# An attention and soft-MoE kernel on one core: norm steps, small operations, turned loads and the order of the last stage rearranged

## The chip, the core and the metric

The kernel runs on one core of a Trainium2 chip. The metric is the device time of one execution in microseconds (us). The kernel before was run three times beside the profile: 319.63, 318.76 and 318.81 us, a median of 318.81 us. Engines go by the names of the profile: PE (TensorE matmuls), PEld (its weight loads), DVE (VectorE), ACT (ScalarE), POOL (GpSimd) and SP (SyncE, which here only issues DMAs).

## What is computed

The inputs are q, k and v of 4 batches, 5056 rows, 256 columns, all fp32, and the weights of a soft mixture of 8 experts with 4 slots each. The attention is over columns: q and k are divided by the norm of each column, and the scores are a 256 x 256 matrix per batch.

```python
qn = q / (np.linalg.norm(q, axis=1, keepdims=True) + 1e-06)
kn = k / (np.linalg.norm(k, axis=1, keepdims=True) + 1e-06)
s = kn.transpose(0, 2, 1) @ qn / tau
a = np.exp(s - s.max(-1, keepdims=True)); a /= a.sum(-1, keepdims=True) + 1e-09
x = (v @ a).reshape(20224, 256)
logits = x @ phi                      # 32 slots
d = softmax(logits, axis=0)           # over all 20224 rows
slot_in = d.T @ x                     # 32 x 256
slot_out[e] = np.maximum(slot_in[e] @ w1[e], 0) @ w2[e]
out = softmax(logits, axis=1) @ slot_out
```

## The kernel before

**Chunks and half chunks.** Each batch's rows are cut into 5 chunks of 1024 rows (the last has 960), and q and k are handled in half chunks of 512 rows: u counts them, 10 per batch, 40 in all. v is handled in whole chunks: y counts those, 5 per batch, 20 in all; y = 12 to 14 are the last three of batch 2 and 15 to 19 are batch 3. In the names of the traces v2_3 is chunk 3 of batch 2.

**Scores (`score`, L194).** For each half chunk, PE adds k'q into a PSUM tile S of the batch. A half chunk has 4 row blocks. In `n_split(u)` of them (L117) q and k are split into a high and a low fp32r part: ACT casts the high part (`cast`, L171), DVE subtracts to get the low part (`split`, L176), and PE runs three fp32r matmuls. The other blocks go to PE as plain fp32 (the profile counts two passes for each of those matmuls). ACT squares the half chunk (`square`, L182) and DVE sums the squares into `all` (`add`, L184 to L192).

**Norms and attention (`attention`, L222).** At a batch's end DVE folds `all` to `sum` (L229, L230), PE sums it over partitions (`nn`, L234), ACT copies the result, POOL takes the root and adds 1e-6 (L244, L245), DVE inverts (L247), POOL multiplies in 1/tau (L250), ACT makes a diagonal matrix `dg`, PE spreads it over partitions (`rq`, L258), and DVE scales a copy of the scores, `ssb` (L264). Then come the row maximum (L267), exp (`a`, L270), a transpose (`aTp`, `aT`) and the product with phi: `Mp`, scaled to `M` (L288, L298). M turns rows of v straight into logits, so no logit of a batch exists before its M.

**Chunks of v (`slots`, L518).** M needs v with its columns on partitions. For that PE transposes half chunks of v (128 columns each; two per chunk, m = 0 and 1): 8 transposes into two PSUM tiles `vTp` (L311), evicted to `vT` by ACT (L322) and in the last stage also by DVE (L320). For 12 of the 40 half chunks (m = 1 of y = 0 to 11) the kernel instead loads a copy of v that the host has laid out with columns first (`load_turned`, L155, tiles vD). PE then makes the logits L (L335), and ACT copies them to `lt` (L346). In the last chunk of a batch DVE first sets rows that don't exist to -1e30 in L itself (L331).

**The running softmax over rows (`chain`, L359).** Per group of 3 or 2 chunks: DVE takes the maximum (L372, or L350 per chunk in batch 3), POOL (DVE in batch 3) folds it over partitions and with the earlier maximum to `negm` (L380 to L401), ACT takes exp (L413), DVE transposes to `dn` (L429), and PE multiplies with v into G (L458). At a batch's end G goes through `a` to `acc` (L478 to L516).

**What sets the order.** The instructions of PE, DVE, ACT and SP stand in the order in which the Python code issues them. A loop over u issues cast, add, score, square and split, and lets generators (`attention`, `slots`, `chain`) take one step at each `advance`; a generator yields the letter of the engine of its next step (E: a big DVE step, one per advance). Chunk y starts at u = LAG + 2y = 16 + 2y. After u = 39 the remaining chunks, y = 12 to 19, are worked off in the same manner, two at a time.

**Loads.** All DMAs are issued by SP in order, so an issue that waits for its buffer holds up all that stand behind it. q and k have 5 raw buffers; v has 6; turned half chunks have 3. From u = 16 on, each chunk of v is issued right behind the half chunks of q and k of the same step. The chunks y = 14 to 18 go into buffers that q and k leave (tag r), then come the weights w1 and w2 of the experts, into buffers that squares, splits and v leave.

**The end.** When batch 3's G is complete, the slots go through the experts (`up` H L691, `flip_h`, `down` O L717), and the output stage (L763 on) multiplies the row softmax with the result, evicts it and stores 20.71 MB.

## Time and profile before

| | us |
|---|---|
| median of three runs | 318.81 |
| the profiled execution's own time | 321.6 |
| its span, first to last instruction | 318.6 |
| PE busy | 291.1 |
| DVE busy | 234.6 |
| ACT busy | 208.2 |
| POOL busy | 49.0 |
| DMA queue, share of 16 engines' span | 85.3% |

The page of a profile sums up one execution. Its windows give, for each stretch, each engine's busy time with the count of instructions, then the granted PE clock (1.00 is full), the mean busy share of the 16 DMA engines, and GB/s. A timeline row gives start, duration, engine, line and names, count, and in brackets the idle time ahead of it and whose result ended it. PE's matmuls are pipelined and their ends are modelled, so the time that a run of matmuls takes is read from the start of one row to the start of the next. Busy time is no proof of a bound: the stage and what is waited for in it decide.

### The profile page before, as it was taken

Reading aid. Unit: us, or ns where it says so; the run is one execution under the profiler, and the core shown is the slowest. Engines: PE = TensorE matmul, PEld = TensorE weight load, DVE = VectorE, ACT = ScalarE, POOL = GpSimd, SP = SyncE. Lnnn points to the kernel's source line nnn. Section 1 sums busy time; section 2 is a strip of 40 time slices with the busy share of each in tenths; the row PEclk is TensorE's granted clock in tenths of the full one; section 3 lists DMA queues with packets and bytes.
Section 4 is the critical chain, followed back from the end, with each engine's and each line's share of the span. In section 5 each row is a group of like instructions: output and inputs, shape, how many; then the busy total and the mean of one; then the engine's idle time right before and its main releaser. Section 6 shows DMA issues by size and latency. Waiting matters only on the chain.

```text
span 318.6 us, 5880 instructions
## 1 busy us (share of the span) xinstructions
PE 291.1 (91%) x2224; PEld 227.2 (71%) x2224; DVE 234.6 (74%) x342; ACT 208.2 (65%) x313; POOL 49.0 (15%) x94
## 2 busy tenths in 40 slices
...
GB/s 294 418 334 348 338 338 255 408 366 413 411 413 384 376 212 419 412 413 388 414 223 236 391 419 400 382 74 338 255 196 422 46 2 263 397 426 399 421 406 292
DMA packets 23468, 106.25 MB, mean 334 GB/s; under 512 B 3216, under 2 KB 4240, under 8 KB 17424
## 3 DMA queue, kind: packets, MB, share of 16 engines
q1 hardware_dynamic: 23440, 105.89, 85.3%
...
q14 instruction: 11, 0.09, 0.1%
HBM read 85.17 MB, written 20.71 MB: 332 GB/s over the span
## 4 chain that ended last, share of the span: by engine, by line
PE 69%; DVE 10%; ACT 7%; issue 5%; DMA 2%; POOL 1%; SPq 1%; ACTq 0%; DVEq 0%; POOLq 0%
PE S L213 33%; PE vTp L311 6%; PE L L335 6%; PE G L458 6%; PE op L786 4%; PE op L787 4%; ACT sq L182 3%; DMA raw<-in_k_dram 2%; PE O L717 2%; PE cTp L775 2%; PE Mp L288 1%; PE nn L234 1%; DVE all L192 1%; DVE nat L650 1%; DVE cm L653 1%
## 5 line engine op out<-in xcount | busy, mean ns | idle before, releaser
L213 PE MATMUL S<-raw 128*128 128x256 f32 x368 | 87.2, 390 | 0.0
L213 PEld LDWEIGHTS S<-raw 128*128 128x128 f32 x368 | 69.4, 194 | 16.1 <-issue 6.1
L182 ACT ACTIVATE sq<-raw 128x2048 f32<-128x2048 f32 x40 | 76.4, 1911 | 4.7 <-DVE all L190 4.7
L192 DVE TENSOR_TENSOR all<-all,sq 128x2048 f32<-128x2048 f32 x32 | 73.1, 2284 | 8.4 <-ACT sq L182 8.2
L176 DVE TENSOR_TENSOR hl<-raw,hl 128x1024 fp32r<-128x1024 f32 (+1 forms) x39 | 42.3, 1085 | 22.0 <-ACT hl L171 22.0
L213 PE MATMUL S<-hl 128*128 128x256 f32 x408 | 56.2, 290 | 1.0 <-DVE hl L176 0.9
L213 PEld LDWEIGHTS S<-hl 128*128 128x128 f32 x408 | 51.1, 191 | 2.6 <-DVE hl L176 1.4
L171 ACT CAST hl<-raw 128x1024 fp32r<-128x1024 f32 (+1 forms) x39 | 36.5, 936 | 17.2 <-PE S L213 9.3
L311 PE MATMUL vTp<-ident,v 128*128 128x128 f32 x224 | 31.0, 285 | 3.9 <-ACT vT L322 3.0
L786 PE MATMUL op<-soh,cT 128*128 128x512 f32 x80 | 32.8, 410 | 0.7 <-ACT cT L780 0.7
L311 PEld LDWEIGHTS vTp<-ident,v 128*128 128x128 f32 x224 | 25.8, 145 | 10.6 <-issue 3.7
L790 ACT COPY o<-op 128x512 f32<-128x512 f32 x53 | 29.0, 606 | 5.4 <-PE op L787 5.4
L787 PE MATMUL op<-sol,cT 128*128 128x512 f32 x80 | 31.6, 395 | 0.0
L322 ACT COPY vT<-vTp 128x512 f32<-128x512 f32 x40 | 21.8, 584 | 14.5 <-PE vTp L311 14.5
L335 PE MATMUL L<-vT,M 128*32 128x256 f32 (+1 forms) x224 | 18.7, 426 | 6.0 <-DVE L L331 4.5
L458 PE MATMUL G<-v,dn 128*32 128x256 f32 x320 | 21.8, 396 | 1.5 <-DVE dn L429 1.5
L792 DVE COPY o<-op 128x512 f32<-128x512 f32 x27 | 18.4, 687 | 4.9 <-PE op L787 4.7
L244 POOL TENSOR_TENSOR rn<-rn,half 128x4 f32<-128x4 f32 x4 | 10.3, 2565 | 60.8 <-ACT rn L243 60.8
L320 DVE COPY vT<-vTp 128x512 f32<-128x512 f32 x16 | 11.0, 689 | 10.1 <-PE vTp L311 9.9
L786 PEld LDWEIGHTS op<-soh,cT 128*128 128x128 f32 x80 | 15.0, 188 | 4.4 <-ACT cT L780 1.4
L787 PEld LDWEIGHTS op<-sol,cT 128*128 128x128 f32 x80 | 15.1, 188 | 3.0
L458 PEld LDWEIGHTS G<-v,dn 128*32 128x32 f32 x320 | 9.5, 112 | 9.9 <-issue 3.1
...
## 6 DMA issues: line engine op xcount, KB each, us to landing
...
v<-in_v_dram SPq DMA_DIRECT2D x16, 1024.0 KB, 10.4
...
```

Of the source, the lines that this page charges most:

```text
L171: nc.scalar.copy(hl[u][:, 0, :, :ns], raw_of(u)[:, :, :ns])
L176: nc.vector.tensor_tensor(hl[u][:, 1, :, :ns], raw_of(u)[:, :, :ns], hl[u][:, 0, :, :ns].bitcast(F32), op=ALU.subtract)
L182: nc.scalar.activation(sq[u], raw_of(u), AF.Square)
L192: nc.vector.tensor_tensor(st[b]["all"], st[b]["all"], sq.pop(u), op=ALU.add)
L213: nc.tensor.matmul(sps[:, m, :], lhs, rhs, start=r == 0 and part == 0 and x == 0 and y == 0 and m == 0, stop=r == H - 1 and part == 1 and ...
L311: nc.tensor.transpose(tp[:, jj, :], vt[:, 4 * hh + jj, P * m : P * m + P], ident)
L322: nc.scalar.copy(dst, st[b]["tp", ch, m, hh])
L335: nc.tensor.matmul(L[S * g : S * g + S, :je, :], M[:, m, :], st[b]["vT", ch, m][:, :je, S * g : S * g + S], start=m == 0, stop=m == 1,)
L458: nc.tensor.matmul(gp[S * g : S * g + S, :], tiles[c][:, j, :], vt[:, j, :], start=c == 0 and j < G, stop=c == n - 1 and j >= G,)
L786: nc.tensor.matmul(op, cT[:, jj, :], soh, start=True, stop=False)
L787: nc.tensor.matmul(op, cT[:, jj, :], sol, start=False, stop=True)
L790: nc.scalar.copy(od, op)
```

## The change

In the order of the program:

- **Splits.** u = 0 and 1 have no split block; from u = 20 on, half chunks with even u have 3 split blocks and odd ones 2 (before: 2 in all of them). Over all u that is 76 instead of 68.
- **Turned loads.** 23 half chunks instead of 12 come turned from memory: both halves of y = 0 to 2, and m = 1 of all others, so also in the last stage. The tiles vD have 4 buffers, and m = 0 of y = 0 to 2 goes into the buffers of vT.
- **Issue order on SP.** Every load has a key in units of u and the list is sorted by it. The first six chunks of v are issued at u = 4, 7, 10, 13, 16 and 19, the later ones at LAG + 2y - 4. Chunks start two half chunks earlier (LAG is 14), so 13 of them start before the scores end.
- **Norms.** DVE's folding of the squares is issued behind the last `add` of its own batch, and `add(u)` follows in the same step u. S is no longer copied: DVE reads it in PSUM, with `rq` as a copy in SBUF. 1/tau sits in the matrix `tones` by which PE spreads `rq`. Of POOL's small steps only the root is left; adding 1e-6 and 1e-9 goes to DVE.
- **Running softmax.** POOL's folding of the maximum goes to DVE, the spreading of `negm` over partitions to ACT, and the two subtractions go into ACT's exp.
- **Rows that don't exist.** POOL writes -1e30 into `lt`, and ACT copies only real rows there. DVE no longer writes to L.
- **The last stage.** `settle` picks the next step by a little model of three engine clocks and of when each generator is ready; PSUM banks for logits and transposes are counted in `busy`, and batch 3 uses a second bank for logits of odd chunks. The five chunks of batch 3 all go into the r buffers, with its turned half chunks and w1_1 to w1_4 between them.

In the diff, TURN gives the halves of chunk y that come turned, LAG the u at which chunk 0 starts, RB the raw buffers, V0 and VS the first key and the spacing of the early loads of v, and LW the w1 loads behind each late chunk.

```diff
+    TURN = lambda y: (0, 1) if y < 3 else (1,)
     VB = 6
     HP = 150
     CUT = [(0, 2), (2, 4), (4, 8)]
     LATE = {2: 1, 3: 6}
-    AHEAD = 0
+    LAG = 14
+    WIDE = 2
+    BIAS = (0, 0, 0, 0)
+    LW = (0, 0, 1, 1, 2)
+    RB = 5
+    LEAD = 4
+    LEADV = 4
+    V0 = 4
+    VS = 3
...
-    NS = 2
+    NS = 3
     H = 2 * NCH
 
     def n_split(u):
-        return 0 if u == 0 else (1 if u < 2 * H and u % 2 else NS)
+        return {0: 0, 1: 0, 2: 1}[u] if u < 3 else (1 if u < 2 * H and u % 2 else 2 if u < 2*H or u%2 else 3)
...
-    def load_qk(b, ch):
-        r = []
...
+    def load_qk(u):
+        b, r = divmod(u, H)
+        ch, h = divmod(r, 2)
+        raw = apool.tile([P, 2, HJ, C], F32, tag="raw", name=f"raw{b}_{ch}_{h}", bufs=RB)
...
-        x = bpool.tile([P, J, P], F32, tag="vD", name=f"vD{b}_{ch}_{m}", bufs=3)
+        x = bpool.tile([P, J, P], F32, tag="vD" if m else "vT", name=f"vD{b}_{ch}_{m}", bufs=4 if m else 3)
...
-        ssb = bpool.tile([P, 2, C], F32, tag="ssb", name=f"ssb{b}")
-        nc.scalar.copy(ssb, st[b]["S"])
-        yield "E"
...
-        nc.gpsimd.tensor_scalar_add(rn, rn, 1e-6)
         yield "D"
+        nc.vector.tensor_scalar_add(rn, rn, 1e-6)
         nc.vector.reciprocal(rn, rn)
-        rk = bpool.tile([P, 2], F32, tag="rk", name=f"rk{b}")
-        for i in range(2):
-            nc.gpsimd.tensor_scalar_mul(rk[:, i : i + 1], rn[:, 2 + i : 3 + i], rtau)
...
-        nc.tensor.matmul(rq[:, :C], ones, dg, start=True, stop=True)
+        nc.tensor.matmul(rq[:, :C], tones, dg, start=True, stop=True)
+        yield "A"
+        rqs = bpool.tile([P, C], F32, tag="dg", name=f"rqs{b}")
+        nc.scalar.copy(rqs, rq[:, :C])
         yield "D" if last else "E"
+        while not st[b].get("scored"):
+            yield "~E"
...
-                ssb[:, m, :], ssb[:, m, :], rk[:, m : m + 1], rq[:, :C], op0=ALU.mult, op1=ALU.mult
+                ssb[:, m, :], st[b]["S"][:, m, :], rn[:, 2 + m : 3 + m], rqs, op0=ALU.mult, op1=ALU.mult
...
-        L = pb.tile([P, 2, J, S], F32, tag="L", name=f"L{b}_{ch}")[:, 0]
+            st[b]["mxs", lo] = bpool.tile([P, 3], F32, tag="mxs", name=f"mxs{b}_{ch}", bufs=2)
+        tag = "amisc" if b == B - 1 and ch % 2 else "L"
+        L = pb.tile([P, 2, J, S], F32, tag=tag, name=f"L{b}_{ch}")[:, 0]
         if ch == NCH - 1:
-            nc.vector.memset(L[TL:, JL, :], -1e30)
+            nc.gpsimd.memset(st[b]["lt", lo][TL:, ch - lo, JL, :], -1e30)
...
-        nc.scalar.copy(st[b]["lt", lo][:, ch - lo], st[b]["L", ch])
+        to, L = st[b]["lt", lo][:, ch - lo], st[b]["L", ch]
+        if ch == NCH - 1:
+            nc.scalar.copy(to[:, :JL], L[:, :JL])
+            nc.scalar.copy(to[:TL, JL], L[:TL, JL])
+        else:
+            nc.scalar.copy(to, L)
...
+    def turn_logits(b, lo, hi):
+        nc.vector.transpose(
+            nat[b][:, lo * J : hi * J, :].rearrange("p j s -> p (j s)"),
+            st[b]["lt", lo][:, : hi - lo].rearrange("p c j s -> p (c j s)"),
+        )
+        run["lt"] -= 1
+        yield from ()
...
-                nc.gpsimd.tensor_scalar_mul(mx[:, g : g + 1], mxs[S * g : S * g + S, 0:1], -1.0)
-        if not final:
-            yield "D"
-        nc.vector.tensor_reduce(mx[:, G:], mx[:, :G], axis=AX.X, op=ALU.min)
+                nc.vector.tensor_scalar_mul(mx[:, g : g + 1], top, -1.0)
...
-            if start:
-                tiny.tensor_copy(to, mx[:, G:])
-            else:
-                tiny.tensor_scalar_min(to, mx[:, G:], before[:S])
+        before, ended = run.get("negm"), run.get("ended")
+        if start:
+            nc.vector.tensor_reduce(negm[:S], mx[:, :G], axis=AX.X, op=ALU.min)
+        else:
+            nc.vector.tensor_reduce(mx[:, G:], mx[:, :G], axis=AX.X, op=ALU.min)
+            nc.vector.tensor_scalar_min(negm[:S], mx[:, G:], before[:S])
         run["negm"] = negm
+        if end:
+            run["ended"] = negm
+        yield "A"
+        for g in range(1, G):
+            nc.scalar.copy(negm[S * g : S * g + S], negm[:S])
...
+            while run["vT"] > 2 or ("T", second_bank(ch)) in busy:
+                yield "~P"
+            bank = "T", second_bank(ch)
+            run["vT"] += 1
+            busy.add(bank)
...
+        if b == B - 1:
+            lo = groups[b][gi][0]
+            scan(b, ch, st[b]["mxs", lo][:, ch - lo : ch - lo + 1])
+            if ch < NCH - 2:
+                to_nat(b, ch)
...
+    def settle(todo, wide):
+        cost = {"P": 0.9, "A": 0.65, "D": 0.6, "E": 1.0}
+        clock = dict.fromkeys("PAD", 0.0)
+        ready = {}
+        spins = 0
+        while todo or active:
+            while todo and sum(x[0] == 2 for x in active) < wide:
+                start_after(slots(*todo.pop(0)), 2, "P")
+            now = min(clock.values())
+            spins = spins + 1
+            assert spins < 3000, [(x[0], x[2].__name__, x[3], x[2].gi_frame.f_lineno, {k: v for k, v in x[2].gi_frame.f_locals.items() if k in ("b", "ch", "gi")}) for x in active]
+
+            def when(x):
+                return max(ready.setdefault(x[1], now), clock["D" if x[3][0] == "E" else x[3][0]])
+
+            x = min(active, key=lambda x: (when(x) + BIAS[x[0]], x[0], x[1]))
+            t, tag, n = when(x), x[3], x[1]
+            if hop(x):
+                ready[n] = t + 0.3
+            else:
+                end = t + (float(tag[1:]) if tag[1:] else cost[tag[0]])
+                clock["D" if tag[0] == "E" else tag[0]] = end
+                ready[n] = end + 0.25
...
+    loads = [(u - RB, 0, load_qk, (u,)) for u in range(B * H)]
+    loads += [(0.5, 1, load_small, ()), (2 * WI, 1, nc.sync.dma_start, (w1t[0], w1[0].rearrange("(p d) f -> p d f", d=2)))]
+    for y in range(NCH * (B - 1)):
+        b, ch = divmod(y, NCH)
+        for m in TURN(y):
+            loads.append((LAG + 2 * y - LEAD + m, 2, load_turned, (b, ch, m)))
+        loads.append((V0 + VS * y if y < VB else LAG + 2 * y - LEADV, 3, load_v, (b, ch)))
+    for key, _, f, args in sorted(loads, key=lambda x: x[:2]):
+        f(*args)
...
+        add(u)
+        if r == H - 1:
+            start_after(attention(b), 0, "E")
         score(u, 0)
         advance("PAD")
-        square(u)
+        if u == 0:
+            square(u)
         if u + 1 < U:
+            square(u + 1)
             split(u + 1)
         score(u, 1)
+        if r == H - 1:
+            st[b]["scored"] = True
...
+    late_w1 = iter(range(1, E))
+    for ch in range(NCH):
+        load_v(b, ch, big("r", f"v{b}_{ch}"))
+        for t in ["w"] * LW[ch]:
+            load_w1(next(late_w1), t)
+        for m in TURN(NCH * b + ch):
+            load_turned(b, ch, m)
+    for e in late_w1:
+        load_w1(e, "v")
...
-        w2t[e] = big(f"w2_{e}")
+        w2t[e] = big("v" if e < E - 5 else "r", f"w2_{e}")
...
-    todo = list(rest)
-    while todo or active:
-        if todo and sum(x[0] == 2 for x in active) < 2:
-            start_after(slots(*todo.pop(0)), 2, "P")
-        advance()
+    settle(list(rest), WIDE)
```

Three places show the move. The first is DVE in batch 2, around u = 22 to 26 (all2 sums squares, hl25 is the split of u = 25, dn0_0 and nat0 are the transposes of batch 0's first group). Before:

```order
L176 TENSOR_TENSOR hl25_981<-raw2_2_1_219,hl25_981 128x1024
L429 STREAM_TRANSPOSE dn0_0_1021<-et0_0_978 128x768
L433 COPY zacc_111<-z0_0_977 128x1
L192 TENSOR_TENSOR all2_883<-all2_883,sq24_1000 128x2048
L283 RECIPROCAL sm1_973<-sm1_973 128x2
L331 MEMSET L0_4_1045 64x32
L176 TENSOR_TENSOR hl26_1027<-raw2_3_0_228,hl26_1027 128x1024
L440 STREAM_TRANSPOSE nat0_106<-lt0_0_717 128x768
```

Now the same stretch reads:

```order
L200 TENSOR_TENSOR all2_855<-all2_855,sq22_889 128x2048
L184 TENSOR_TENSOR hl23_904<-raw2_1_1_224,hl23_904 128x2x512
L272 SCALAR_TENSOR_TENSOR ssb1_949<-S1_519,rn1_837,rqs1_902 128x256 x2
L275 TENSOR_REDUCE nm1_951<-ssb1_949 128x2
L200 TENSOR_TENSOR all2_855<-all2_855,sq23_928 128x2048
L184 TENSOR_TENSOR hl24_969<-raw2_2_0_227,hl24_969 128x1536
L291 TENSOR_SCALAR sm1_952<-sm1_952 128x2
L292 RECIPROCAL sm1_952<-sm1_952 128x2
L379 STREAM_TRANSPOSE nat0_107<-lt0_0_663 128x768
```

The MEMSET of L0_4, which stood behind an addition of squares, is gone from DVE, and the splits of even u have 1536 elements a row instead of 1024.

The second is PE from the norm sums of batch 3 (nn3) on. Before:

```order
L234 MATMUL nn3_1824<-ones_84,sum3_1759 128x1 x4
L311 MATMUL vTp2_2_0_0_1830<-ident_79,v2_2_307 128x128 x4
L311 MATMUL vTp2_2_0_1_1835<-ident_79,v2_2_307 128x128 x4
L487 MATMUL gtp1_1844<-fold_96,gs1_1671 128x32 x2
L311 MATMUL vTp2_2_1_0_1850<-ident_79,v2_2_307 128x128 x4
L311 MATMUL vTp2_2_1_1_1855<-ident_79,v2_2_307 128x128 x4
L311 MATMUL vTp2_3_0_0_1860<-ident_79,v2_3_309 128x128 x4
L311 MATMUL vTp2_3_0_1_1865<-ident_79,v2_3_309 128x128 x4
L311 MATMUL vTp2_3_1_0_1886<-ident_79,v2_3_309 128x128 x4
L311 MATMUL vTp2_3_1_1_1891<-ident_79,v2_3_309 128x128 x4
L258 MATMUL rq3_1896<-dg3_1874,ones_84 128x256
L511 MATMUL sp1_1898<-a1_971,gts1_1877 32x256 x2
```

Now:

```order
L239 MATMUL nn3_1800<-ones_84,sum3_1796 128x1 x4
L324 MATMUL vTp2_3_0_0_1877<-ident_79,v2_3_318 128x128 x4
L324 MATMUL vTp2_3_0_1_1882<-ident_79,v2_3_318 128x128 x4
L324 MATMUL vTp2_4_0_0_1903<-ident_79,v2_4_322 128x128 x4
L324 MATMUL vTp2_4_0_1_1908<-ident_79,v2_4_322 128x128 x4
L260 MATMUL rq3_1916<-dg3_1897,tones_105 128x256
L471 MATMUL G2_0_1922<-v2_0_291,dn2_0_1913 32x256 x8
L349 MATMUL L2_3_1935<-vT2_3_0_1900,M2_1569 32x256 x4
L349 MATMUL L2_3_1935<-vD2_3_1_320,M2_1569 32x256 x4
L471 MATMUL G2_0_1922<-v2_1_301,dn2_0_1913 32x256 x8
L349 MATMUL L2_4_1962<-vT2_4_0_1919,M2_1569 32x256 x2
```

Between nn3 and the first products G2_0 stood sixteen tiles of transposes, and M of batch 3 (Mp3); now four tiles stand there, and Mp3 comes behind G2_0. nn3 still stands behind the last score matmul of its batch.

The third is SP, the last loads of batch 1. Before:

```order
L141 DMA raw1_3_1_176<-in_q_dram 128x1024
L141 DMA raw1_3_1_176<-in_k_dram 128x1024
L159 DMA vD0_0_1_179<-in_v_rows_dram 128x1024
L152 DMA v0_0_181<-in_v_dram 128x2048
L141 DMA raw1_4_0_183<-in_q_dram 128x1024
L141 DMA raw1_4_0_183<-in_k_dram 128x1024
L141 DMA raw1_4_1_186<-in_q_dram 128x768
L141 DMA raw1_4_1_186<-in_q_dram 64x256
L141 DMA raw1_4_1_186<-in_k_dram 128x768
L141 DMA raw1_4_1_186<-in_k_dram 64x256
L159 DMA vD0_1_1_192<-in_v_rows_dram 128x1024
L152 DMA v0_1_194<-in_v_dram 128x2048
```

Now:

```order
L150 DMA raw1_2_1_175<-in_k_dram 128x1024
L167 DMA vD0_0_0_178<-in_v_rows_dram 128x1024
L160 DMA v0_2_180<-in_v_dram 128x2048
L150 DMA raw1_3_0_182<-in_q_dram 128x1024
L150 DMA raw1_3_0_182<-in_k_dram 128x1024
L167 DMA vD0_0_1_185<-in_v_rows_dram 128x1024
L150 DMA raw1_3_1_187<-in_q_dram 128x1024
L150 DMA raw1_3_1_187<-in_k_dram 128x1024
L167 DMA vD0_1_0_190<-in_v_rows_dram 128x1024
L150 DMA raw1_4_0_192<-in_q_dram 128x1024
L150 DMA raw1_4_0_192<-in_k_dram 128x1024
L167 DMA vD0_1_1_195<-in_v_rows_dram 128x1024
```

These rows held two turned half chunks and two chunks of v; now they hold four and one, and v0_0 and v0_1 stand further up, between loads of batches 0 and 1. A raw load is still issued when the raw buffer of five half chunks earlier comes free, and everything that stands ahead of it is moved first.

166 lines of the change are left out of this document (66 added, 100 removed).

## The prediction

> **What bounds the kernel now.** I read the windows first, cut at the stage ends that PE's timeline shows: scores of batches 0 to 3, the last chunks, the experts, the output. A row gives the stretch and its length, busy time (and instructions) of PE, PEld, DVE, ACT and POOL, the granted clock, the DMA share and GB/s.
>
> ```profile
> 0.00:41.00 41.00, 38.39 (x191) 32.23 (x192) 28.64 (x28) 27.50 (x23) 1.22 (x7) 1.00 0.92 347
> 41.00:81.00 40.00, 39.45 (x262) 35.07 (x261) 34.01 (x27) 31.94 (x38) 9.22 (x7) 1.00 0.94 358
> 81.00:132.10 51.10, 49.23 (x391) 40.35 (x390) 40.26 (x38) 39.80 (x52) 13.93 (x24) 0.97 0.96 372
> 132.10:187.30 55.20, 53.60 (x464) 42.28 (x463) 43.44 (x43) 39.94 (x54) 17.01 (x29) 1.00 0.92 354
> 187.30:241.90 54.60, 46.03 (x480) 31.26 (x478) 31.47 (x92) 20.45 (x57) 7.65 (x27) 0.91 0.74 292
> 241.90:259.00 17.10, 16.71 (x210) 7.81 (x211) 12.32 (x25) 6.67 (x11) 0.00 (x0) 1.00 0.35 146
> 259.00:318.60 59.60, 47.74 (x242) 38.15 (x241) 44.42 (x94) 41.86 (x80) 0.00 (x0) 0.94 0.86 348
> ```
>
> Up to 187.3 PE is busy 96 to 99% of four stages and the DMA engines 92 to 96%: PE bounds, with the loads close behind. From 187.3 to 241.9 nothing is full: this stage waits. From 241.9 on the change touches nothing of weight, so I carry 318.6 - 241.9 = 76.7 us over.
>
> Next, what a step costs PE. These rows of PE's timeline are one half chunk and its neighbours in batch 2.
>
> ```profile
> 88.08 3.72 PE L213 MATMUL S<-raw 128*128 128x256 f32 x16
> 91.64 1.04 PE L311 MATMUL vTp<-ident,v 128*128 128x128 f32 x8
> 92.43 3.12 PE L213 MATMUL S<-hl 128*128 128x256 f32 x24
> 95.39 0.59 PE L258 MATMUL rq<-dg,ones 128*128 128x256 f32 x2
> 95.91 0.64 PE L335 MATMUL L<-vT,M 128*32 128x256 f32 x8
> 96.36 0.61 PE L335 MATMUL L<-vD,M 128*32 128x256 f32 x8
> 96.91 3.72 PE L213 MATMUL S<-raw 128*128 128x256 f32 x16
> ```
>
> From start to start, 16 plain passes take 3.56 us (0.2225 each), 24 split matmuls 2.96 (0.123), the transposes of a half chunk 0.79, the logits of a chunk 1.00.
>
> Then the waits in that stage: first two rows of DVE, then five of PE.
>
> ```profile
> 104.06 2.29 DVE L192 TENSOR_TENSOR all<-all,sq 128x2048 f32<-128x2048 f32 x1
> 106.44 0.09 DVE L331 MEMSET L<- 64x32 f32 x1
> ...
> 106.67 1.05 PE L335 MATMUL L<-vT,M 128*32 128x256 f32 x8 [1.87 <-DVE L L331]
> 107.42 1.16 PE L335 MATMUL L<-vD,M 128*32 128x224 f32 x8
> 108.50 2.78 PE L213 MATMUL S<-raw 128*128 128x256 f32 x8
> 111.12 0.97 PE L288 MATMUL Mp<-phi_sb,aT 128*128 128x32 f32 x8
> 161.61 0.62 PE L335 MATMUL L<-vT,M 128*32 128x256 f32 x8 [1.60 <-DVE L L331]
> ```
>
> A memset of 0.09 us stood behind an addition of 2.29 us, and PE waited 1.87 us for it, 1.60 us again in the next batch. After the first wait 108.50 - 106.67 = 1.83 us went on logits that cost 1.00 elsewhere, and 2.62 on 8 plain passes that cost 1.78: 1.7 us of slow clock.
>
> **Stage one, to the norm sums of batch 3 (187.3 before).**
> - Splits: 76 blocks instead of 68. That is 32 plain passes less (7.1 us) and 48 split matmuls more (5.9): -1.2 on PE.
> - Chunks: 13 instead of 12 fall into the stage, so +1.0 of logits; transposed half chunks fall from 12 to 10 (y = 0 to 2 need none): -1.6.
> - The memset goes to POOL and into lt, and PE no longer waits for DVE there: -(1.87 + 1.60 + 1.7) = -5.1. What is late next there is the eviction of lt by ACT, which PE's following logits need a whole half chunk later.
> - More on DVE and ACT. From u = 20 on, the split of even u grows from 1024 to 1536 elements:
>
> ```profile
> L176 DVE TENSOR_TENSOR hl<-raw,hl 128x1024 fp32r<-128x1024 f32 x29 | 35.5, 1223 | 15.1 <-ACT hl L171 15.1
> L176 DVE TENSOR_TENSOR hl<-raw,hl 128x512 fp32r<-128x512 f32 x10 | 6.9, 686 | 6.9 <-ACT hl L171 6.9
> L391 DVE TENSOR_SCALAR negm<-mx,negm 32x1 f32<-32x1 f32 x8 | 1.6, 204 | 0.2
> ```
>
> 512 elements more cost 1.223 - 0.686 = 0.54 us. Per batch the small steps taken over from POOL are some twelve at 0.204: 2.4 us. A pair of half chunks in batch 3 has 43.44/5 = 8.7 us of DVE; now 8.7 + 0.54 + 0.5 = 9.7. PE's pair is 3.56 + 2.96 + 0.79 + 1.00, 1.00 for G, and some 0.8 for attention (estimated from matmuls like the seven rows above), 10.1, now 9.95 by 12 plain passes and 30 split matmuls. DVE still fits, with 3% left, so some of its waits will reach PE: bounds 0 (it fits) and +5 (0.5 us on each of the ten pairs). I take +1, near the lower end, because squares now stand a half chunk ahead of their additions. ACT, at 39.94/5 = 8.0, has room for what it gets.
> - Loads that are late. Of the share-weighted rates, 358/0.94 = 381, 372/0.96 = 388 and 354/0.92 = 385: 385 GB/s is what the engines moved when full. Up to the half chunk u = 24 SP now issues 25 x 1.05 MB of q and k, 5 chunks of v and 7 turned halves of 0.52, 35.1 MB: 91 us at that rate, and 3 for the idle 8% of the first 41 us, so 94. Its cast stands at the start of half chunk 23, the second half of the split matmuls from 92.43: 93.9, less 3 x 0.79 is 91.5. Late by 2.5. Bounds: 0 at 400 GB/s, +7.7 at 365. Later in the stage a pair asks 3.67 MB per 10 us, 367 GB/s, and the lead grows again.
>
> Sum: -1.2 + 1.0 - 1.6 - 5.1 + 1 + 2.5 = -3.4, so 183.9.
>
> **The last chunks (54.6 us before).** This view is PE, ACT and DVE on the way to M, then to the experts.
>
> ```profile
> 190.06 0.18 DVE L247 RECIPROCAL rn<-rn 128x4 f32<-128x4 f32 x1
> 193.72 0.86 DVE L264 SCALAR_TENSOR_TENSOR ssb<-ssb,rk,rq 128x256 f32<-128x256 f32 x2
> ...
> 201.96 2.55 PE L311 MATMUL vTp<-ident,v 128*128 128x128 f32 x12 [1.77 <-ACT vT L322]
> 204.30 1.75 PE L288 MATMUL Mp<-phi_sb,aT 128*128 128x32 f32 x8
> 230.75 1.06 PE L335 MATMUL L<-vT,M 128*32 128x256 f32 x16 [1.00 <-DVE L L331]
> 241.86 5.36 PE L691 MATMUL H<-w,slT 128*32 128x512 f32 x48 [0.30 <-DVE slT L669]
> 253.51 5.39 PE L717 MATMUL O<-w,hT 128*32 128x256 f32 x96
> ...
> 206.09 0.47 ACT L298 ACTIVATE M<-Mp,sm 128x32 f32<-128x32 f32 x2 [1.81 <-PE Mp L288]
> ```
>
> The clock in it, in two windows, and the length of three steps:
>
> ```profile
> 204.00:208.00 4.00, 3.91 (x27) 2.62 (x25) 2.12 (x5) 0.76 (x4) 0.53 (x1) 0.50 0.61 252
> 208.00:212.00 4.00, 3.59 (x33) 1.40 (x33) 1.16 (x3) 0.73 (x2) 1.29 (x6) 0.50 0.01 4
> ```
>
> ```profile
> L429 DVE STREAM_TRANSPOSE dn<-et 128x768 f32<-128x768 f32 x3 | 2.9, 971 | 0.0
> L270 ACT ACTIVATE a<-ssb,nm 128x256 f32<-128x256 f32 x8 | 4.0, 503 | 0.6 <-DVE nm L267 0.6
> L413 ACT ACTIVATE et<-lt,negm 128x768 f32<-128x768 f32 x3 | 2.8, 935 | 4.8 <-POOL negm L391 2.9 <-POOL negm L389 1.9
> ```
>
> - To M: 206.5 - 187.3 = 19.2 us. nn still stands behind the last score and the root is still on POOL: rn inverted at 190.06 - 187.3 + 0.18 = 2.9, now 2.6 with one hop less. dg ends at 3.5, rq at 4.0. DVE has dn (0.97), nat (0.97) and two evictions of vT (0.69) ahead of ssb, so it starts at 6; ssb 0.9, nm 0.7 and a 1.1 end at 8.7. On ACT the eviction of L2_3, that of L2_4, and behind a new maximum the exp of batch 2's second group stand ahead of aT: 14.2. aT 0.6, Mp 0.8, M 0.5: 16.2 instead of 19.2, so -3. Less PE work is in the way, but ACT's queue takes its place.
> - M to the last logits: 231.8 - 206.5 = 25.3. Of 16 transposed half chunks in the whole stage 7 are left. Behind M now stand two products G (1.00 each, like logits), five logits, three transposed half chunks (2.4) and 1 of small matmuls: 10.4, plus 3.6 for evictions, above all vT of the last half chunk, which ACT takes behind three exps. 14: -11.
> - Last logits to H: 10.1, the same chain; one memset wait less: -0.5.
> - Clock: after the wait of 1.77 the clock stood at 0.50 for 8 us, so 4 us were lost. Two waits of that size remain (for the eviction of L, and for aT). Bounds 0 and +5; I take +2.5, since half of the slow work lies under waits.
>
> 54.6 - 3 - 11 - 0.5 + 2.5 = 42.6: H starts at 183.9 + 42.6 = 226.5, and 226.5 + 76.7 = 303.2.
>
> **The floor of the loads.** From the page:
>
> ```profile
> HBM read 85.17 MB, written 20.71 MB: 332 GB/s over the span
> ```
>
> Eleven more turned halves (two of 0.49) make 90.9 MB. At 385 GB/s, 236 us and 3: w2_7 is there at 239. PE's second round of `down`, the last 64 of the 96 matmuls from 253.51, started at about 255.3; now it would at 226.5 + 13.4 = 239.9. Both meet. With 1 us for the landing, 240 + 3.6 for these matmuls + 59.7 to the end = 303.3. I take 303.3 for the span, 15.3 less than 318.6. The profiled execution took 321.6, 0.9% above the median of 318.81; taking the difference off the median gives 303.5.
>
> **The rivals.**
> 1. **The loads bind (20%).** At 372 GB/s, the best average of the four stages, w2_7 comes at 247.4 + 1, the span is 311.7: 312. For: the four stages together never moved more. Against: there SP waited for v's buffers, which the spread loads avoid:
>
> ```profile
> SPq L152 <- PE G L458: 18.9, 5, 6.6
> 120.00:140.00 20.00, 20.00 (x179) 15.75 (x179) 14.34 (x13) 14.48 (x20) 0.31 (x1) 1.00 1.02 415
> ```
>
> 2. **Slower: reads at the rate of the last score stage (9%).** The change pays in loads for what it saves on PE. At 354 GB/s throughout, 90.9 MB take 256.8 + 3; the second round of `down` starts at 260.8 instead of 255.3, the span is 324.1: 324. It decides at 90.9/(255.3 - 4) = 362 GB/s: below that the kernel is slower, whatever PE does. For: three of four stages stayed under it. Against: they weren't asked for more, with 415 over 20 us when they were. [...]
> 3. **The order of the last stage only trades waits (8%).** M and the evictions queue on ACT and DVE, and the stage stays at 54: span 183.9 + 54 + 76.7 = 314.6, so 315.
> 4. **It changes nothing (4%).** Late loads and DVE take 7 + 5 in stage one, and the last stage gains 4.6 only: 183.9 - 3.5 + 12 + 50 + 76.7 = 319.
> 5. **Better (7%).** No late loads, no slow clock, 400 GB/s: w2_7 at 230.3, PE's path 180.4 + 40.1 + 76.7 = 297.2: 297.5.
>
> **The numbers.** My case has 52% (300 to 308 us). The range reaches from 298, where rival 5 begins, to 315, which takes in rivals 1 and 3; about 2 in 10 stay outside. About 0.3%, 1 us, can be told from no change. Faster: 52 + 20 + 8 + 7 = 87%; same 4%; slower 9%.
>
> **What would show it.** Right: no wait of PE at the fifth chunk's logits; the norm sums of batch 3 near 184; M some 16 us behind; 7 transposed half chunks after that; H near 226; DMA share near 1.0 from 25 us on. Wrong: PE waiting for raw loads around u = 20 to 26, or for w2 in the second round of `down`; hl waits on DVE beyond 0.5 us per pair; a gap at 0.50 clock as long as before.

## The result, and the profile after

The changed kernel took 308.99 us (median of four, 307.38 to 309.69) against 318.78 us for the kernel before on the same chip (median of four): a ratio of 0.9683, 95% interval 0.964 to 0.9725. It is faster by 9.8 us where 15.3 were forecast; the time lies inside the range of 298 to 315. Six more times on another chip gave 310.19 us (308.57 to 312.18), ratio 0.9752 (0.9701 to 0.9802); the median of all ten is 309.3.

Two more numbers are needed to read this. The profiled execution of after is the fastest of the ten (307.38 us, span 305.1, mean granted clock 0.981; the other nine are at 0.955 to 0.968). The profiled execution of before, from which every step of the prediction was taken (321.6 us, span 318.6), was at 0.968, the lowest clock that any of its executions had. The ratios leave out executions more than 1.5% above the fastest of their kernel; without them the kernel before has medians of 316.5, 316.5 and 318.6 us beside the three groups of experiments below.

The windows of after, at its own stage ends, with the columns of those of before:

```profile
41.00:83.50 42.50, 39.47 (x262) 33.73 (x261) 35.53 (x32) 31.32 (x36) 1.92 (x4) 1.00 1.02 396
83.50:134.30 50.80, 50.80 (x441) 41.34 (x440) 45.74 (x52) 43.36 (x60) 1.96 (x4) 1.00 1.01 394
134.30:185.30 51.00, 51.00 (x442) 41.51 (x441) 45.22 (x54) 38.90 (x58) 1.96 (x4) 1.00 0.95 365
185.30:227.53 42.23, 31.32 (x378) 21.36 (x376) 23.29 (x77) 18.03 (x62) 2.49 (x5) 0.96 0.96 390
227.53:238.00 10.47, 10.47 (x86) 3.69 (x90) 7.45 (x16) 4.79 (x8) 0.00 (x0) 0.84 0.99 408
238.00:245.60 7.60, 7.60 (x129) 4.46 (x121) 5.42 (x11) 1.98 (x4) 0.00 (x0) 1.00 0.05 19
245.60:305.10 59.50, 47.48 (x246) 38.43 (x242) 44.45 (x92) 41.96 (x80) 0.00 (x0) 0.96 0.86 349
```

PE is busy without a break from 83.5 to 185.3. The last stage is 42.2 us long instead of 54.6, and the DMA engines are full through it (0.96) and nearly to 238. The page's line on memory gives the amount that was forecast:

```profile
HBM read 90.87 MB, written 20.71 MB: 366 GB/s over the span
```

PE's timeline of after, with the rows that answer to the waits of before: two waits of batch 0 and 1, the fifth chunk's logits of batches 2 and 3 (102.06 and 152.99), and the last stage.

```profile
54.89 0.93 PE L287 MATMUL aTp<-ident,a 128*128 128x128 f32 x4 [1.28 <-ACT a L279]
...
79.48 0.64 PE L349 MATMUL L<-vD,M 128*32 128x256 f32 x8 [1.16 <-DMA vD<-in_v_rows_dram]
...
102.06 0.60 PE L349 MATMUL L<-vT,M 128*32 128x256 f32 x8
...
152.99 0.60 PE L349 MATMUL L<-vT,M 128*32 128x256 f32 x8
...
185.32 0.95 PE L239 MATMUL nn<-ones,sum 128*128 128x1 f32 x8
...
199.95 1.08 PE L297 MATMUL Mp<-phi_sb,aT 128*128 128x32 f32 x8 [2.09 <-ACT aT L290]
...
216.88 0.63 PE L349 MATMUL L<-vT,M 128*32 128x256 f32 x8 [3.71 <-DVE vT L332]
...
227.53 7.05 PE L744 MATMUL H<-w,slT 128*32 128x512 f32 x48 [0.30 <-DVE slT L722]
```

The waits of 1.87 and 1.60 us for the memset are gone. New are 1.28 us for `a` and 1.16 us for a turned half chunk, and in the last stage 3.71 us for the eviction of the last transposed half chunk (the largest now), and H takes 7.05 us for 48 matmuls that took 5.36 in the profile of before (6.91 in a second one, below).

PE's groups by line up to the norm sums of batch 3 (busy time and mean, then idle time ahead of them), in after and then in a second profile of before:

```profile
L221 PE MATMUL S<-raw 128*128 128x256 f32 x336 | 78.5, 385 | 0.1
L221 PE MATMUL S<-hl 128*128 128x256 f32 x456 | 62.7, 290 | 2.2 <-DVE hl L184 2.2
L324 PE MATMUL vTp<-ident,v 128*128 128x128 f32 x80 | 10.7, 277 | 0.0
...
L524 PE MATMUL sp<-a,gts 128*32 128x256 f32 x8 | 2.1, 385 | 0.0
```

```profile
L213 PE MATMUL S<-raw 128*128 128x256 f32 x368 | 85.9, 386 | 0.0
L213 PE MATMUL S<-hl 128*128 128x256 f32 x408 | 56.4, 290 | 1.5 <-DVE hl L176 1.5
L311 PE MATMUL vTp<-ident,v 128*128 128x128 f32 x96 | 12.7, 275 | 0.0
...
L511 PE MATMUL sp<-a,gts 128*32 128x256 f32 x4 | 1.1, 385 | 0.0
```

Eight matmuls of vTp are a half chunk: 10 instead of 12. `sp` stands here twice instead of once: the last steps of batch 1 moved into this stage.

### The profile page after: what moved, and what is told of

It is laid out like the page before. It is cut to its first block, busy times and chain, and to the rows that moved or that the text cites. A ratio compares the mean times of both kernels' runs of the same rounds, so it can differ in the third digit from the quotient of the medians.

```text
span 305.1 us, 5685 instructions
## 1 busy us (share of the span) xinstructions
PE 275.8 (90%) x2152; PEld 216.2 (71%) x2152; DVE 236.7 (78%) x356; ACT 209.1 (69%) x327; POOL 9.6 (3%) x24
## 4 chain that ended last, share of the span: by engine, by line
PE 68%; DMA 9%; DVE 8%; ACT 8%; issue 3%; SPq 1%; POOL 1%; ACTq 0%; POOLq 0%; DVEq 0%
PE S L221 31%; PE L L349 5%; PE G L471 5%; PE op L839 5%; PE vTp L324 5%; PE op L840 5%; DMA v<-in_v_dram 4%; PE H L744 3%; DMA vD<-in_v_rows_dram 3%; PE cTp L828 2%; PE O L770 2%; DMA raw<-in_k_dram 2%; ACT sq L190 2%; DVE all L198 1%; PE nn L239 1%
## 5 line engine op out<-in xcount | busy, mean ns | idle before, releaser
L221 PE MATMUL S<-raw 128*128 128x256 f32 x336 | 78.5, 385 | 0.1
L221 PEld LDWEIGHTS S<-raw 128*128 128x128 f32 x336 | 62.6, 191 | 13.4 <-issue 5.3
L221 PE MATMUL S<-hl 128*128 128x256 f32 x456 | 62.7, 290 | 2.2 <-DVE hl L184 2.2
L179 ACT CAST hl<-raw 128x1024 fp32r<-128x1024 f32 (+2 forms) x38 | 39.7, 1044 | 20.5 <-PE S L221 13.4
L184 DVE TENSOR_TENSOR hl<-raw,hl 128x1024 fp32r<-128x1024 f32 (+2 forms) x38 | 46.3, 1219 | 3.8 <-ACT hl L179 3.6
L324 PE MATMUL vTp<-ident,v 128*128 128x128 f32 x136 | 19.1, 284 | 1.7 <-DVE vT L332 1.7
L324 PEld LDWEIGHTS vTp<-ident,v 128*128 128x128 f32 x136 | 15.8, 148 | 5.2 <-issue 2.9
L334 ACT COPY vT<-vTp 128x512 f32<-128x512 f32 x27 | 14.7, 585 | 2.9 <-PE vTp L324 2.8
L833 ACT CAST cT<-cTp 128x512 fp32r<-128x512 f32 x20 | 11.5, 593 | 6.8 <-PE cTp L828 6.8
L198 DVE TENSOR_TENSOR all<-sq,sq 128x2048 f32<-128x2048 f32 x4 | 9.1, 2268 | 8.7 <-ACT sq L190 8.7
L349 PE MATMUL L<-vT,M 128*32 128x256 f32 (+1 forms) x136 | 11.2, 390 | 4.6 <-DVE vT L332 3.7
```

What stands on the lines that cost most here:

```text
L179: nc.scalar.copy(hl[u][:, 0, :, :ns], raw_of(u)[:, :, :ns])
L184: nc.vector.tensor_tensor(hl[u][:, 1, :, :ns], raw_of(u)[:, :, :ns], hl[u][:, 0, :, :ns].bitcast(F32), op=ALU.subtract)
L221: nc.tensor.matmul(sps[:, m, :], lhs, rhs, start=r == 0 and part == 0 and x == 0 and y == 0 and m == 0, stop=r == H - 1 and part == 1 and ...
L324: nc.tensor.transpose(tp[:, jj, :], vt[:, 4 * hh + jj, P * m : P * m + P], ident)
L349: nc.tensor.matmul(L[S * g : S * g + S, :je, :], M[:, m, :], st[b]["vT", ch, m][:, :je, S * g : S * g + S], start=m == 0, stop=m == 1,)
```

## The experiments

All times are in us; n counts executions. The kernel before ran beside each group on one chip: 318.27 (n 7) for the first three rows, 316.87 (n 17) for the next four, 318.7 (n 11) for the last four. The changed kernel itself ran beside the last group only; across groups, medians carry the spread of the clock with them (0.968 to 0.989 in the executions of before), so the ratio to before and the traces count for more there.

| kernel | median (n) | least to most | ratio to before, 95% |
|---|---|---|---|
| before, with the memset part alone | 312.13 (4) | 311.84 to 316.17 | 0.9875 (0.977 to 0.998) |
| after, memset part undone | 310.71 (4) | 308.58 to 311.93 | 0.979 (0.969 to 0.989) |
| after, order of the tail undone | 309.03 (4) | 308.58 to 310.12 | 0.9753 (0.968 to 0.982) |
| after, turned loads undone | 314.69 (10) | 313.3 to 316.89 | 0.9969 (0.993 to 1.001) |
| after, early attention undone | 311.63 (4) | 309.27 to 313.01 | 0.9846 (0.979 to 0.991) |
| after, more split blocks | 310.72 (4) | 308.58 to 311.53 | 0.9815 (0.976 to 0.987) |
| after, two waits in the order | 305.81 (6) | 303.8 to 310.45 | 0.9648 (0.959 to 0.971) |
| after, unchanged | 310.19 (6) | 308.57 to 312.18 | 0.9752 (0.970 to 0.980) |
| before, with memset and turned loads | 323.05 (6) | 319.7 to 325.12 | 1.0123 (1.006 to 1.019) |
| after, spread of v undone | 308.94 (4) | 306.85 to 310.22 | 0.9706 (0.964 to 0.977) |
| two waits, two turned loads fewer | 309.1 (6) | 307.49 to 309.51 | 0.9709 (0.967 to 0.975) |

**The kernel before, profiled again.**

> The kernel before, unchanged, profiled a second time. The prediction took its steps from one profiled execution of 321.6 us (span 318.6), 0.9% above the median of 318.81, and took the difference of 15.3 off the median. Theory A: that execution was an ordinary slow draw (in the trace of after the spans lie between 305.1 and 307.4 at granted clocks of 0.981 to 0.960), so a second profile shows a time of 318 to 320 and a span of 315 to 317, with less idle or a higher clock spread over the stages; the steps would then have been measured from a start some 2 to 3 us too late. Theory B: a profiled execution of the kernel before is always some 0.9% longer, and this one shows 321 to 322 again.

It took 319.81 us, span 317.3, clock 0.973: theory A's time, with a span 0.3 above its 315 to 317. It is near the top of the 36 times of before that the experiments gave, this one included (314.06 to 321.17, median 317.96). Over those, span and clock go together: 312.1 to 313.5 us at 0.988 and 0.989, 318.4 to 319.4 at 0.968. So the starting point was an ordinary draw, but one from the end of a spread of 7 us that one profile doesn't show.

**The memset alone, in the kernel before.**

```diff
-            nc.vector.memset(L[TL:, JL, :], -1e30)
+            nc.gpsimd.memset(st[b]["lt", lo][TL:, ch - lo, JL, :], -1e30)
...
-        nc.scalar.copy(st[b]["lt", lo][:, ch - lo], st[b]["L", ch])
+        to, L = st[b]["lt", lo][:, ch - lo], st[b]["L", ch]
+        if ch == NCH - 1:
+            nc.scalar.copy(to[:, :JL], L[:, :JL])
+            nc.scalar.copy(to[:TL, JL], L[:TL, JL])
+        else:
+            nc.scalar.copy(to, L)
```

> The kernel before with one part of the change alone: the memset of the fifth chunk's padding goes to POOL and into lt, and the last chunk's eviction copies only the real rows. Theory A (the prediction's term): PE no longer waits 1.87 and 1.60 us behind the additions on DVE and loses no slow clock after it, 5.1 us in all and 0.5 in the last stage: 313.5 us, ratio 0.984. Theory B: PE's wait is only slack that the next wait takes (for the split, or for the loads, at 0.92 to 0.96 of the DMA engines in those stages): 317.5 to 319, ratio 0.996 to 1. In between, 315 to 316, the waits of 3.5 us go and the slow clock is not theirs.

312.13 us, 4.4 less than the 316.5 of before beside it. The ratio of 0.9875 holds theory A's 0.984, but its interval, 0.977 to 0.998, leaves 0.7 to 7 us of gain and touches theory B's 0.996. At the same clock the gain is smaller: three of the four executions had 0.989 or 0.990 and spans of 309.6 to 310.4, and before at 0.988 and 0.989 took 312.1 to 313.5: medians of 310.1 and 312.4, some 2 us. That the memset also brought the better clock isn't shown. The trace says the same: against the second profile of before, the norm sums of batch 3 come 186.13 - 183.30 = 2.8 us earlier, the two waits without slow clock. The last stage, in which the part removes a wait of 1.0 us, is 3.4 shorter, and what follows 1.5, and both of these are mostly clock: from the norm sums to H it was 0.93 in the second profile of before and 1.00 here, and in the experts 0.92 and 1.00. These are the stage and one wait in it, in the second profile of before and in this kernel:

```profile
186.13:239.09 52.96, 44.41 (x477) 30.55 (x473) 31.48 (x92) 20.51 (x57) 7.61 (x27) 0.93 0.78 303
```

```profile
200.81 2.45 PE L311 MATMUL vTp<-ident,v 128*128 128x128 f32 x12 [1.77 <-ACT vT L322]
```

```profile
183.30:232.88 49.58, 41.49 (x473) 28.59 (x473) 31.09 (x90) 20.62 (x59) 7.74 (x28) 1.00 0.81 318
```

```profile
197.98 1.58 PE L311 MATMUL vTp<-ident,v 128*128 128x128 f32 x12 [1.77 <-ACT vT L322]
```

The same wait of 1.77 us for the same eviction: behind it 12 transposes took 2.45 us in one (2.55 in the first profile of before) and 1.58 in the other, whose clock stayed at 1.00; in the second profile of before it was 0.66 from 200 to 204 us and 0.50 from 204 to 208. What a wait costs in clock is not fixed. It also means that much of the last stage before was clock: at 1.00 it takes 49.6 us, not 54.6.

**The memset undone, in after.** The edit is the reverse of the one above.

> The changed kernel with this one part undone: DVE's memset into L and the whole eviction again. Theory A: PE waits again behind the additions at the fifth chunk of batches 2 and 3, 1.6 to 1.9 us each with slow clock behind it, and 0.5 in the last stage: 3 to 5 us over 309, so 312 to 314 us, ratio 0.98 to 0.985. Theory B: with the squares a half chunk ahead of their additions DVE comes to the memset in time, and nothing is lost: 308.5 to 310, ratio 0.967 to 0.973.

310.71 us against 309.3: 1.4 more, inside the spread of after, and with an interval (0.969 to 0.989) that takes in both theories; the trace decides. In batches 2 and 3 PE doesn't wait for the memset at all, and in the last stage hardly longer than after does for ACT at the same place (0.89 us). DVE's rows at the fifth chunk of batch 2, and PE's there and in the last stage:

```profile
99.77 2.28 DVE L200 TENSOR_TENSOR all<-all,sq 128x2048 f32<-128x2048 f32 x1
102.06 0.09 DVE L345 MEMSET L<- 64x32 f32 x1
```

```profile
103.00 0.60 PE L349 MATMUL L<-vT,M 128*32 128x256 f32 x8
...
195.30 0.63 PE L349 MATMUL L<-vT,M 128*32 128x256 f32 x8 [1.06 <-DVE L L345]
...
218.00 1.07 PE L349 MATMUL L<-vT,M 128*32 128x256 f32 x8 [3.81 <-DVE L L345]
```

The 3.81 us at 218.00 is the wait of 3.71 for the eviction that after has too. So theory B for the waits, but not for its reason: the memset still stands right behind an addition of 2.28 us. It ends at 102.15, and PE comes to these logits only at 103.00, behind a product G (102.12) that the new order has put ahead of them. The memset's new place and the new order each take this wait away, so the two gains don't add.

**The order of the tail undone.**

```diff
-    settle(list(rest), WIDE)
+    todo = list(rest)
+    while todo or active:
+        if todo and sum(x[0] == 2 for x in active) < 2:
+            start_after(slots(*todo.pop(0)), 2, "P")
+        advance()
```

> The changed kernel with the loop of the kernel before for the last stage: every part that is active is advanced in turn, instead of the part that is ready. Theory A: the order by readiness gives a good part of the last stage's gain (42.2 us from the norm sums to the experts, 54.6 before): this kernel comes to 313 to 316 us, ratio 0.98 to 0.99, with PE waiting for M and for evictions of vT behind work of other parts. Theory B: the gain comes from the fewer transposed half chunks and the attention that starts earlier, and the order hardly counts: 308 to 310.5 us, ratio 0.965 to 0.974.

309.03 us: theory B. No gain of the tail ordered by readiness shows here; its waits only stand elsewhere (for aT, for the spreading of `negm`, for `dn`), and the stage is 41.0 us long, after's 42.2.

```profile
201.75 1.08 PE L297 MATMUL Mp<-phi_sb,aT 128*128 128x32 f32 x8 [1.99 <-ACT aT L290]
...
215.80 0.63 PE L349 MATMUL L<-vT,M 128*32 128x256 f32 x8 [1.62 <-ACT negm L413]
...
221.85 1.93 PE L471 MATMUL G<-v,dn 128*32 128x256 f32 x32 [2.21 <-DVE dn L443]
```

**The turned loads undone.**

```diff
-    TURN = lambda y: (0, 1) if y < 3 else (1,)
+    TURN = lambda y: (1,) if y < 12 else ()
...
-        run["vT"] -= (ch, 0) not in st[b]["turned"]
+        run["vT"] -= sum((ch, m) not in st[b]["turned"] for m in range(2))
```

> The changed kernel with the turned loads of v undone: 12 half chunks are loaded turned as before, one in each of the first twelve chunks, instead of 23; PE transposes 11 half chunks more and the loads carry 5.7 MB less. Theory A (the prediction's count): each transposed half chunk costs PE 0.79 us; two of them fall into the score stages (+1.6), nine into the last stage, of which some hide in PE's idle 10.9 us of 42.2: in all +5 to +8, so 314 to 317 us, ratio 0.985 to 0.995. Theory B: the last stage is set by waits for DVE and ACT, the transposes lie inside them, and lighter loads give something back: 308.5 to 310.5 us, ratio 0.966 to 0.974.

314.69 us, 5.4 more than after: theory A. By the ratio it is more, since 0.9969 is no gain over before that can be told; and at the same clock, 0.979 to 0.981, the spans are 311.6 to 312.5, 6.5 to 7.4 above the 305.1 of after. The split of it is another than expected. Four of the eleven half chunks, not two, fall into the score stages, because 13 chunks now start there:

```profile
L324 PE MATMUL vTp<-ident,v 128*128 128x128 f32 x112 | 15.0, 277 | 0.0
```

The norm sums of batch 3 come at 190.98 (185.32 and 187.00 in the two profiles of after). The other seven half chunks lengthen the last stage to 45.0 from 42.2 and 43.4, by 1.6 to 2.8 us, where seven at 0.79 would be 5.5. How many of them lie in waits stays open, since this stage had a clock of 1.00 here and of 0.96 and 0.88 in after.

```profile
190.98 1.05 PE L239 MATMUL nn<-ones,sum 128*128 128x1 f32 x8
...
235.95 5.36 PE L744 MATMUL H<-w,slT 128*32 128x512 f32 x48 [0.30 <-DVE slT L722]
```

The 45.0 us also show what else made this stage shorter: 14 of before's 16 transposed half chunks still stand in it. From 54.6 us in the first profile of before, 5.0 went with the memset part and its full clock (49.6), 4.6 with the rest of the change, which leaves one chunk fewer for the stage, and 2.8 with the turned loads, though after's slower clock hides up to 0.04 x 42.2 = 1.7 more.

**The early attention undone.**

```diff
-        if r == H - 1:
-            start_after(attention(b), 0, "E")
+        if r == 0 and b > 0:
+            start_after(attention(b - 1), 0, "E")
+            st[b - 1]["scored"] = True
```

(For the last batch it starts behind the loop.)

> The changed kernel with the first part of the change undone: the attention of a batch is started in the next batch's first step, as before, and not with the batch's last half chunk, so that the norms are not ready with the scores. Theory A: M of batch 3 comes 19 us behind its norm sums instead of 16.2, and the stage behind it is later by as much, 2 to 4 us: 311 to 313 us, ratio 0.975 to 0.983. Theory B: ACT's queue sets M, not the norms, and the early start gives nothing: 308 to 310 us, ratio 0.966 to 0.973. Less than that would mean that the early start crowds DVE or ACT at a batch's end.

311.63 us, 309.27 to 313.01, which overlaps with after's 307.38 to 312.18: the medians differ by 2.3, a loss that these runs don't settle. What they settle is M. The product with phi starts 201.33 - 186.71 = 14.62 us behind the norm sums, in after 199.95 - 185.32 = 14.63, behind the same wait:

```profile
186.71 0.95 PE L239 MATMUL nn<-ones,sum 128*128 128x1 f32 x8
...
201.33 1.82 PE L297 MATMUL Mp<-phi_sb,aT 128*128 128x32 f32 x8 [2.09 <-ACT aT L290]
```

So theory B for M: what ACT has queued sets it, as the prediction had it, and not the norms.

**More split blocks.**

```diff
-2 if u < 2*H or u%2 else 3)
+2 if u < 2*H else 3)
```

> The changed kernel with three split blocks in every half chunk of batches 2 and 3, instead of three in even and two in odd ones: ten blocks more, each with 4 plain passes less and 6 split matmuls more on PE (0.15 us less) and 0.54 us more on DVE. It measures the crowding of DVE, which the prediction put at +1 with bounds 0 and +5. Theory A: DVE, at 9.0 us of a pair's 10.2, still fits at 9.6 and PE gets its 1.5 us: 307 to 308.5 us, ratio 0.962 to 0.969. Theory B: DVE has no room, its splits and evictions come late, and PE waits 0.3 to 0.5 us per pair: 311 to 314 us, ratio 0.975 to 0.985, with hl or lt named in PE's waits of batches 2 and 3.

310.72 us, between the two. From batch 1's norm sums to those of batch 3 PE took 100.7 us (101.0 in after), so it got 0.3 of its 1.5; what the median lies above after's comes behind these batches. DVE fits, at 47.38 and 46.89 us in five pairs:

```profile
85.00:135.00 50.00, 49.62 (x447) 40.64 (x447) 47.38 (x51) 43.91 (x59) 1.97 (x4) 1.00 1.00 385
135.00:185.30 50.30, 49.74 (x449) 40.77 (x448) 46.89 (x52) 40.96 (x59) 1.95 (x4) 1.00 0.97 372
```

PE waited once in each of the two batches, for `dn` (DVE's transpose for G), 0.38 and 0.56 us; no wait for hl or lt there. DVE is nearly full with 9.5 us of a pair's 10, and not above it.

**Two waits more in the order of issue.**

```diff
         yield "A"
+        while final and not end and ("vT", NCH - 1, 0) not in st[b]:
+            yield "~A"
+        while end and b == B - 2 and "M" not in st[B - 1]:
+            yield "~A"
         for g in range(1, G):
             nc.scalar.copy(negm[S * g : S * g + S], negm[:S])
```

> The changed kernel with two waits more in the order of issue: the exps of batch 3's first group are issued behind the eviction of its last transposed half chunk, and the exp of batch 2's second group behind M of batch 3. In the trace of after, PE waits 3.71 us for that eviction and 2.09 us for aT, each queued behind exps on ACT and what follows them on DVE. Theory A: most of these two waits goes and the time with it, 2 to 4 us: 305 to 307 us, ratio 0.955 to 0.962. Theory B: the next wait (the products behind the exps, which now start later) or the loads of w2 take its place: 308 to 310 us, ratio 0.965 to 0.972; PE's wait then shows dn or gs, or w.

305.81 us, least 303.8, the lowest times and the lowest ratio in the table: theory A by the time, the border of the two by the ratio of 0.9648. How much it gains over after is not settled, since the two never ran side by side and after's ratios, 0.968 and 0.975, have intervals that overlap with its 0.959 to 0.971. What the trace shows is that M comes 2.4 us earlier, the waits of 2.09 and 3.71 are gone and the stage is 38.1 us long, after's 42.2 and 43.4. Then the loads are next:

```profile
211.98 0.93 PE L349 MATMUL L<-vD,M 128*32 128x256 f32 x8 [2.25 <-DMA vD<-in_v_rows_dram]
...
223.32 5.36 PE L748 MATMUL H<-w,slT 128*32 128x512 f32 x48 [0.30 <-DVE slT L726]
...
239.98 3.64 PE L774 MATMUL O<-w,hT 128*32 128x256 f32 x58 [1.84 <-DMA w<-in_moe_w_dram]
```

PE waits 2.25 us for a turned half chunk, and 1.84 us for the weights of the second round of `down`, until 239.98. H takes 5.36 us again. But it took 6.91 in the second profile of before, which has no wait above 1.77 us in this stage, so that the wait of 3.71 makes H slow isn't shown:

```profile
239.09 6.91 PE L691 MATMUL H<-w,slT 128*32 128x512 f32 x48 [0.30 <-DVE slT L669]
```

**The changed kernel again.**

> The changed kernel unchanged, on the chip of the three kernels below, so that they are compared with it side by side. Its first four times were 307.4 to 309.7 us at granted clocks of 0.981 to 0.960. Expected: 308 to 310 us, ratio 0.965 to 0.978, and a clock that stays below that of the best runs of before (0.989), if the wait of 3.71 us for an eviction costs it clock each time.

310.19 us, clocks 0.955 to 0.968: as expected. Whether the wait of 3.71 us is the reason stays open: behind it the logits took 1.07 us here, and 0.63 in the first profile. The rows of this profile (span 308.5) are the norm sums of batch 3, the long wait and H.

```profile
187.00 0.95 PE L239 MATMUL nn<-ones,sum 128*128 128x1 f32 x8
...
218.57 1.07 PE L349 MATMUL L<-vT,M 128*32 128x256 f32 x8 [3.71 <-DVE vT L332]
...
230.40 7.05 PE L744 MATMUL H<-w,slT 128*32 128x512 f32 x48 [0.30 <-DVE slT L722]
```

**Memset and turned loads alone, in the kernel before.** 22 half chunks turned; three buffers for them, as before, and the buffers of vT for the evictions.

```diff
+    TURN = lambda y: (0, 1) if y < 3 else (1,) if y < 19 else ()
...
+        for m in TURN(y):
+            loads.append((LAG + 2 * y - 4 + m, 2, load_turned, (y // NCH, y % NCH, m)))
+        loads.append((LAG + 2 * y - 4, 3, load_v, (y // NCH, y % NCH)))
...
     for x, ch in rest[PRE:]:
         load_v(x, ch, big(f"v{x}_{ch}"))
+        if (x, ch) != (B - 1, NCH - 1):
+            load_turned(x, ch, 1)
```

> The kernel before with two parts of the change alone: the memset on POOL into lt, and half chunks of v loaded turned, 22 of the change's 23 (the last chunk's isn't), with the loads of q, k and v in the order of before. The early attention, the small steps on VectorE and ScalarE, the spread of v, the finer splits and the order of the tail are all as before. Theory A: these two parts are the whole gain (6 and 5.7 us when done or undone alone), the rest is worth nothing or costs something: 306 to 309 us, ratio 0.963 to 0.973. Theory B: the other parts are what lets the turned loads pay (v spread thinly, four buffers for the turned halves): here SP waits for buffers, PE for loads, and the time stays at 310 to 314 us, ratio 0.977 to 0.99.

323.05 us: slower than before by 1.2% (0.6 to 1.9). Neither range; it goes theory B's way, and further. PE's waits by what ended them, and the windows:

```profile
PE O L716 <- DMA w<-in_moe_w_dram: 4.6, 3, 1.9
PE L L336 <- DMA vD<-in_v_rows_dram: 4.4, 3, 2.2
PE L L336 <- ACT vT L323: 3.1, 1, 3.1
```

```profile
145.30:191.70 46.40, 45.83 (x392) 36.10 (x390) 38.58 (x38) 34.16 (x49) 18.84 (x29) 1.00 0.92 353
...
250.00:256.00 6.00, 2.38 (x26) 0.88 (x18) 1.04 (x2) 0.00 (x0) 0.00 (x0) 0.88 0.66 276
```

The DMA engines were busy 0.92 of the time in batches 2 and 3 while the loads were behind, PE waited 4.4 us for three turned half chunks between 69 and 90 us, and the last weights w2 arrived only at 256, behind three waits of together 4.6 us in `down`. The first expert products started at 234.5, earlier than in either profile of before, and 4 to 7 us behind after's; from there to the end it took 88.1 us instead of 77 to 78. Not all of the loss is loads: the wait of 3.1 us is for an eviction into vT, and the clock was 0.88 from 250 to 256 us and 0.55 from there to 262. In these runs the turned loads pay only with the rest of the change; which of it (the fourth buffer, chunks that start two half chunks earlier, the issue order) was not tried one by one.

**The spread of v undone.**

```diff
-        loads.append((V0 + VS * y if y < VB else LAG + 2 * y - LEADV, 3, load_v, (b, ch)))
+        loads.append((LAG + 2 * y - LEADV, 3, load_v, (b, ch)))
```

> The changed kernel with the spread of v's first chunks undone: each chunk of v is asked for four half chunks ahead of its use, as the later ones are. Theory A: the loads meet in the second half chunks of batches 0 and 1, SP waits for v's buffers (in before 18.9 us in five waits) while the DMA engines stand still, and PE waits 2 to 5 us more than the 1.16 us it now waits for a turned load at 79.5: 311 to 314 us, ratio 0.978 to 0.99. Theory B: there is slack enough in the five buffers of q and k: 308 to 310 us, ratio 0.965 to 0.975.

308.94 us beside after's 310.19: theory B. SP's waits (total, count, longest), here and then in after, are the same for the turned buffers:

```profile
SPq L167 <- PE L L349: 29.8, 5, 8.8
```

```profile
SPq L167 <- PE L L349: 30.0, 5, 8.7
```

**Two turned loads fewer, on the kernel with the two waits.**

```diff
-    TURN = lambda y: (0, 1) if y < 3 else (1,)
+    TURN = lambda y: (0, 1) if y < 3 else (1,) if y not in (15, 16) else ()
...
-        run["vT"] -= (ch, 0) not in st[b]["turned"]
+        run["vT"] -= sum((ch, m) not in st[b]["turned"] for m in range(2))
```

> The kernel with the two waits in the order of issue (305.8 us), with two turned loads of the last stage taken back (the first two chunks of batch 3 are transposed by PE again). In its trace PE waited 2.25 us for a turned half chunk and 1.84 us for w2 in the second round of the product with w2, at 238 to 240 us: the loads are its floor there, where the prediction put it. Theory A: 1.05 MB less bring both 2.7 us earlier, the two transposed half chunks (1.6 us) lie where PE waited: 302.5 to 304.5 us, ratio 0.947 to 0.957. Theory B: the evictions of these two halves stand in the way of M or of the exps and the gain is spent: 305.5 to 307.5 us, ratio 0.957 to 0.967.

309.1 us: above theory B's range too. It ran on another chip than the kernel that it starts from, and the intervals of the two ratios overlap, so the loss isn't settled by the times. The traces show what happened: the waits for loads are gone, but the two half chunks to transpose and evict put waits for `dn` in their place, and the stage from the norm sums to H is 40.3 us long instead of 38.1:

```profile
217.23 2.80 PE L475 MATMUL G<-v,dn 128*32 128x256 f32 x48 [1.83 <-DVE dn L447]
222.24 1.93 PE L475 MATMUL G<-v,dn 128*32 128x256 f32 x32 [2.21 <-DVE dn L447]
```

So here work that must pass ACT and DVE was no free filling where PE waited for a load.

## Why the prediction was right and wrong

**What was right.** The sign, that turned loads pay in this kernel, and that PE's waits for the memset go. PE's work up to the norm sums of batch 3 changed as counted: against the second profile of before, 85.9 - 78.5 = 7.4 us less of plain passes (7.1 forecast), 62.7 - 56.4 = 6.3 more of split matmuls (5.9), 12.7 - 10.7 = 2.0 less of transposes (1.6). The 1.7 us of slow clock behind one of the waits for the memset, part of the same term, stand in the first profile of before only; the second has none there. M was there 16.2 us behind the norm sums (201.06 + 0.47 - 185.32, ACT's row of after), and for the reason given, ACT's queue: without the early attention the product ahead of it starts at the same place, and in the kernel with the two waits, where batch 2's exp stands behind it, it comes at 198.66 + 0.47 - 185.23 = 13.9.

```profile
201.06 0.47 ACT L307 ACTIVATE M<-Mp,sm 128x32 f32<-128x32 f32 x2 [0.41 <-PE Mp L297]
```

The loads ended near 238, where the floor put them at 239. In the kernel with the two waits, PE stood until 239.98 for w2, and the floor with its 1 us for the landing said 240; no run shows that 1 us by itself, and by an estimate from the windows of this kernel it was too short: the engines' share was 1.01 from 220 to 230 us, 0.82 from 230 to 240 and 0.00 from 240 to 246, so at the full share the loads ended near 238, some 2 us before PE went on.

**What came out right by luck.** The last stage took 42.2 where 42.6 was forecast, H started at 227.53 (226.5). But from M to the end of the last logits it took 16.4 us and not 14, and the 2.5 put down for slow clock filled that up. And of the 8.9 us that this step did lose, 3.3 were slow clock and the memset wait (it takes 22.0 in the kernel with the memset part, at 1.00), 2.8 came with the rest of the change (19.2 with the turned loads undone, at 1.00) and only 2.8 with the turned loads.

**The miss of 5.5 us, step by step.** It is 3.4 us of span (306.7 is the median span of the first four, 303.3 was forecast) and 2.1 us in the last step.

- The last step failed: "taking the difference off the median". It set the time only 0.2 us above the span of 303.3. Time and span differ by 3.0 us in the profile of before and by 2.3 in those of after, so the same span would have been 305.6. The difference was taken from an execution at a clock of 0.968, the lowest of before, and put on the median of executions that mostly had a better one. At 0.968 itself, spans of before were 318.4 to 319.4 and two of after 306.7 and 306.8, so 12 us.
- Of the span, 1.4 us came before the norm sums of batch 3 (185.32, forecast 183.9): the omitted step. The products `gtp` and `sp` of batch 1 moved into this stage from behind it, 1.0 us by the rows of `sp` above and 0.5 of `gtp`. The forecast's 3.5 us for crowding and late loads had the right size by luck: 0.7 us more of waits for hl, 1.3 for `a`, 1.2 for a turned half chunk. The wait for `a` is that of batch 0, whose attention now starts early (0.30 us where that is undone). PE never waited for a raw load around u = 20 to 26, and batches 2 and 3, where I had put the crowding, have no wait at all.
- The last stage came 0.4 shorter than forecast.
- Behind H, 76.7 us were carried over; it took 77.6, and 78.1 in the second profile. In the second profile of before it took 78.2, so 76.7 was a draw as well. H itself took 7.05 us instead of 5.36.
- The rest, 1.6 us from the first profile's 305.1 to the median span, goes with the clock again, 0.981 against 0.955 to 0.968. The forecast gave the slow clock of the last stage 2.5 us; there it was 0.96 in the first profile and 0.88 in the second, which is up to 0.12 x 43.4 = 5.2 us. Nine of after's ten executions lie at or below the lowest clock of before, and why is not known.

One reading of the prediction is off without consequence: in the first of the four stages PE was busy 38.39 of 41 us, 94% and not 96.

**The parts' shares.** The turned loads stand out: 5.4 us when undone, more by the ratio and at the same clock. The memset alone is worth 0.7 to 7 us by its ratio, some 2 at the same clock, and in after its new place is not needed, since the new order takes the wait away too. The rest of the change shows no gain by itself: with the turned loads undone it makes 314.7 together with the memset (311.0 us of span at 0.987), where the memset alone makes 312.1 (309.6 to 310.4 at 0.989 and 0.990; the intervals of their ratios overlap). The order of the tail by readiness shows none either; rival 3, that this only trades waits, is right for that part. The stage as a whole became shorter, by the clock and the rest of the change more than by the turned loads.

**Rivals 1 and 2.** The loads hardly bound in after: from 41 to 238 us the engines moved 365 to 408 GB/s, and PE waited for them once, 1.16 us. But rival 2's mechanism exists: in the kernel with memset and turned loads alone PE waited 9 us for turned half chunks and weights, and it lost 1.2%, with 90.38 MB that took until some 254 us (0.66 of the window from 250 to 256), 356 GB/s.

**What stays open.** Which part of the change lets the turned loads come in time; which part shortens the last stage beyond the transposes; whether the early attention is worth 2 us or nothing; why the clock drops behind one wait and not behind its twin, and why after is granted less of it than before (0.955 to 0.981 against 0.968 to 0.989).
